# Linear attention and a gated convolution FFN on one core: one batch's q transposed on TensorE, one convolution moved to VectorE, a new order

## The chip, the cores and the metric

The kernel runs on 1 core of a Trainium2 chip. The metric is the device time of one execution in microseconds. Runs are compared by their median; the profile is of one further execution, and its span runs from the first to the last instruction.

## The reference

For each of 8 batches and 8 heads (576 tokens, 64 dims) linear attention without a softmax is computed, normed over the head dim, and all heads of a batch become one 576 x 512 matrix that goes through a gated FFN with a convolution over the tokens:

```python
kv  = einsum('bhsd,bhse->bhde', k, v)
out = einsum('bhsd,bhde->bhse', q, kv)
x   = out / sqrt(mean(out*out, -1) + 1e-6) * g_norm      # -> x[b, s, h*64+d], 512 wide
h   = maximum(x @ w_in, 0)                               # 512 -> 1024
c   = w0*h[s-1] + w1*h[s] + w2*h[s+1]                    # per feature, zero at the ends
y   = (h * sigmoid(c)) @ w_out                           # 1024 -> 512
```

Inputs and outputs are fp32 in HBM; the matmuls take bf16.

## The kernel before

All work is written as small steps, and one long text, `ORDER` (L67), lists the 690 of them. A loop (L797) calls each step in that order, and a chain of dependencies at the end (L807) keeps the instructions of each engine in it. So `ORDER` is the queue of every engine at once: a step that stands ahead of another is ahead of it on the engine that they share. What follows `@` are the buffer slots that the step takes (for PSUM, the first of the eight banks), and a `:1` moves a copy to the other of ScalarE and VectorE: for most steps no mark means ScalarE and `:1` VectorE, for `qc` and `qc0` it is the other way round.

The steps that matter here, with batch b first and token, head pair t, half u, feature block f or row block m behind it:

- `Lq`, `Lk`, `Lv` (L301) load and cast one batch on GpSimd's queue, two slots for each of q, k and v, so a load waits until the batch before last has been read. `Li` and `Lo` load quarters of w_in and halves of w_out. `pl` (L273) sets a selection matrix on GpSimd.
- `kv` (L349) multiplies k by v on TensorE; `kvc`, `kvn`, `ky` copy the result out of PSUM, `kx` by a transfer.
- q has to lie with the head dim on the partitions. Batches 0 to 3 transpose it on TensorE (`qt0`, `qt`; L380 in the rows); batch 4, the only one in `QP`, does so two tokens at a time (`qtp`, 12 products by the identity for each half, L388), and `qc` copies the result from PSUM. Batches in `QD` (5, 6, 7) use a transposing transfer instead, `dq` (L436), issued by SyncE: two for each batch.
- `ot` and `oq` multiply q by kv; `sq` squares on ScalarE, `oc` copies to fp32. Norms: batches 0 and 1 by `on`, `nl`, `mu0` (L562); the others by `ss` (L575), `ln`, `sl` on VectorE, `sp` (L603) and `mu` (L629), whose result is x. `fw` and `fr` bring batch 7's factors through HBM.
- `hm` (L640) is x @ w_in for one batch and 128 features, eight products of 288 columns; `ha` and `hb` are its two halves for features 2 and 3 of batch 1. `re` is the relu, on ScalarE (L646) or VectorE (L648).
- The convolution works in groups `CONV` (L64): 0 and 1 are batches 0 and 1 alone, 2, 3 and 4 two batches each. On VectorE it is `ta` (two scaled copies of h, L699 and L700), `aa` (their shifted sum, L706) and `ab` (plus h, L712), for two features at a time, in one of two `taps` buffers of two batches' size; a one-batch group leaves half of its buffer empty. On TensorE it is `cm` (L731): six products with diagonal matrices `dgw` that `dg` made. `sg` (L745 after `ab`, L742 after `cm`) is the sigmoid on ScalarE, `mg` (L751) multiplies h by it on VectorE.
- `om` (L761) is the product with w_out for 128 rows, in two halves for the pairs of batches in `SPLIT`; `ea` copies the row out, `st` stores it from SyncE's queue.
- `unread.n` and fill counts (L427) multiply a constant tile n times into a bank that nobody reads.

ScalarE loads an activation table ten times, wherever `ORDER` changes between norm steps and sigmoids.

In the order before, group 0 and group 1 do features 6 and 7 with `cm` and the other six on VectorE.

Of the kernel before, what the change touches and what calls it, by code (L numbers as in the profile page):

```python
# [67 lines left out]
pre@0,0,0 unread.10@0 qt0.0.0@0 ps pn pi ca.k.0 ca.v.0 kv.0.0.1@1 kvc.0.0.1.0:1@0 ct@2 qt0.0.1@3 qc0.0.0:1@0  # L68
kvc.0.0.1.1 ot.0.0@0 qc0.0.1:1 unread.3@4 kv.0.1.1@3 Lq.1.0@1 pg sq.0.0@0 on.0.0@4 al.x0@0 al.h1@0 nl.0.0@0 pc
dg.7:1 kvc.0.1.1.0:1 dg.6:1 unread.1@6 qt0.0.2@2 kvc.0.1.1.1:1 ot.0.1@6 unread.3@3 kv.0.2.1@3 sq.0.1@1 mu0.0.0  # L70
al.x1@1 Li.1 al.h0@1 kvc.0.2.1.0:1 Li.3 qc0.0.2:1@1 kvc.0.2.1.1:1 on.0.1@4 nl.0.1@1 qt0.0.3@2 Lv.1.0@1 ot.0.2@0
mu0.0.1 sq.0.2@2 qc0.0.3:1 unread.3@3 kv.0.3.1@4,5 kvc.0.3.1.0 on.0.2@6 kvc.0.3.1.1:1 nl.0.2@2 ot.0.3@4 mu0.0.2
sqh.0.3.0@3 unread.3@3 onh.0.3.0@6 sqh.0.3.1 onh.0.3.1 nlh.0.3.0@3 muh.0.3.0 Lk.1.0@1 qt.1.0@0 nlh.0.3.1 qc.1.0:1@2
muh.0.3.1 Li.0 hm.0.2@6 re.0.2 ta.0.2@0 hm.0.3@4 re.0.3 hm.0.6@6 Lq.1.2 ta.0.3 Lv.1.2 re.0.6 aa.0.1 hm.0.7@4 Lk.1.2
Lq.2.0@0 cm.0.6@6 re.0.7:1 sg.0.6@1 kv.1.0.2@0 cm.0.7@4 kvc.1.0.2.0:1@1 kvc.1.0.2.1 sg.0.7 ot.1.0@0 hm.0.1@6 ab.0.1
sq.1.0@4 re.0.1 qt.1.1@4 hm.0.0@2 on.1.0@6 mg.0.3 qc.1.1@3 ot.1.1@4 nl.1.0@4 re.0.0:1 sq.1.1@5 kv.1.2.2@2
kvc.1.2.2.0 ta.0.0@1 mu0.1.0 kvc.1.2.2.1 on.1.1@6 Li.2 ot.1.2@2 nl.1.1@5 ot.1.3@0 ta.0.1 sq.1.2@6 mu0.1.1 aa.0.0
# [5 lines left out]
sq.2.2@1 sg.0.4 oc.2.2@1 sg.0.5 sq.2.1@2 Lo.1 Lq.4.0@0 Lq.5.0@1 qc.3.0@2 ta.1.5 ot.2.3@4 re.1.1:1 sq.2.3@3 hm.1.0@6
oc.2.1 Lk.4.0@0 Lv.4.0@0 kv.3.0.4@2 re.1.0 ss.2@3 oc.2.3 mg.0.2 ln.8@0 aa.1.2 kvc.3.0.4.0:1@1 kvc.3.0.4.1:1 ab.1.2
unread.3@0 ot.3.0@4 ta.1.0@1 ot.3.1@6 sq.3.0@4 ot.3.2@0 ta.1.1 al.x2@0 oc.3.0@2 aa.1.0 sq.3.2@5 oc.3.2@3 sq.3.1@6
om.0.3.0@2 om.0.0.0@3 oc.3.1 sl.8@0 om.0.1.0@4 ot.3.3@0 om.0.1.4 ab.1.0 om.0.3.4 sq.3.3@7 oc.3.3 sp.2.1@6,0 ss.3@5
dq.5.0@3 ea.0.1@0 mu.2.1.0 Lk.5.0@1 mu.2.1.1 om.0.0.4 ea.0.3@1 ln.1@0 sp.2.0@4,6 mu.2.0.1 mu.2.0.0 dq.5.1@0
# [5 lines left out]
st.0.0 ab.2.2 ta.2.6@0 sg.2.5 re.3.1 re.3.2 ta.2.7 oq.4.3@6 oq.4.2@0 sg.2.4 re.2.3 kv.5.0.4@5 sq.4.2@2 Lv.7.0@0
Lk.7.0@0 om.0.6.4 om.0.5.0@2 aa.2.3 ab.2.3 Lk.6.0@1 Lv.6.0@1 kvn.5.0.4 sq.4.3@3 oc.4.2@0 mg.2.2 ky.5.0.4.0:1
ea.0.6@4 ss.4@3 dq.7.0@1 oc.4.3 ky.5.0.4.1:1 oq.5.0@0 oq.5.1@4 sq.5.0@4 ta.2.2@1 om.0.5.4 sq.5.1@5 oc.5.0:1@2
om.0.4.0@6 oc.5.1 ta.2.3 oq.5.3@0 oq.5.2@4 aa.2.1 om.0.8.0@7 ea.0.5@5 ab.2.1 sq.5.3@6 om.0.4.4 sq.5.2@7 ss.5 ln.2@0
om.0.8.4 hm.2.1@2 oc.5.2@3 ea.0.8@6 oc.5.3 re.2.1 sl.2@0 hm.2.0@4 sp.4.1@0,2 ea.0.4@7 om.0.7.0@7 re.2.0 mu.4.1.0
mu.4.1.1 sp.4.0@4,0 kv.7.0.4@6 mu.4.0.0 sg.2.2 mu.4.0.1 om.0.7.4 kvn.7.0.4:1 sg.2.3 ea.0.7@2 sp.5.0@4,2 hm.3.0@0
al.h2@1 re.3.0 kx.7.0.4.0 dq.7.1@4 mu.5.0.1 mu.5.0.0 hm.4.5@2 re.4.5 sp.5.1@6,4 hm.4.1@0 mg.2.1 mu.5.1.0 hm.4.2@2
mu.5.1.1 ta.2.0@1 sg.2.7 hm.4.0@6 hm.5.3@4 ta.2.1 re.4.1 sg.2.6 mg.2.3 kx.7.0.4.1 re.4.0 re.4.2 oq.7.0@0 re.5.3  # L100
kv.6.0.4@6 oq.7.1@4 sq.7.0@0 hm.5.2@2 oc.7.0@1 aa.2.0 Lq.6.0@1 hm.4.3@0 st.0.4 dq.6.0@2 sq.7.1@1 oc.7.1 re.5.2
hm.4.4@4 st.0.5 kvn.6.0.4:1 ab.2.0 ta.3.2@0 re.4.3 hm.5.6@0 st.0.1 ta.3.3 hm.5.4@2 hm.5.1@6 sg.2.1 sg.2.0 re.4.4
# [22 lines left out]
def kernel(  # L125
# [567 lines left out]
    @op  # L693
    def ta(c, f):
        h, n = span(c)
        if f % 2 == 0:
# [2 lines left out]
        nc.vector.tensor_scalar_mul(tap[:, 0, f % 2, :n, 8:8 + S], h[:, f], cwn[:, 0, f:f + 1])  # L699
        nc.vector.tensor_scalar_mul(tap[:, 1, f % 2, :n, :S], h[:, f], cwn[:, 2, f:f + 1])  # L700
# [145 lines left out]
```

## Time and profile before

| | us |
|---|---|
| median of 3 runs | 179.97 (179.6 to 180.15) |
| profiled execution, first to last instruction | 177.6 |
| the median over that span | 2.4 |
| last matmul ends, from the span's start | 174.3 |
| TensorE busy | 168.4 |
| ScalarE busy | 149.7 |
| VectorE busy | 139.5 |
| GpSimd busy | 30.8 |

No time of its own is listed for the profiled execution beside its span; the 2.4 us are what the timed runs have around it. In the rows PE is TensorE's matmul, PEld its weight load, DVE VectorE, ACT ScalarE, POOL GpSimd, SP SyncE. An engine's instructions overlap at their ends, so busy times are less than sums of durations. The granted TensorE clock is 1.000 in the mean. The loads keep the transfer engines busy until about 100 us.

### The profile page before, as it was taken

To read this page: it belongs to the slowest core of one execution; us is meant where nothing else is said; L and a number is where in the kernel's file an instruction comes from. 1 tells how busy PE (TensorE), PEld (TensorE's weight loads), DVE (VectorE), ACT (ScalarE), POOL (GpSimd) and SP (SyncE) were. 2 spreads that over 40 slices of the span, in tenths; PEclk is the share of its full clock that TensorE was granted. 3 is DMA by queue.
4 is the path that set the end of the run, shared out by engine and by line. 5 is a ranking of instruction groups with operands and counts; after the bars stand their busy time and mean duration, and the time that the engine had idled before them with its cause. 6 is when DMAs were issued, how large, how long until landed. Compare 5 with 4: busy or idle time off the path is not lost.

```text
span 177.6 us, 4060 instructions
## 1 busy us (share of the span) xinstructions
PE 168.4 (95%) x1641; PEld 101.3 (57%) x1660; DVE 139.5 (79%) x235; ACT 149.7 (84%) x233; POOL 30.8 (17%) x54
## 2 busy tenths in 40 slices
...
GB/s 155 188 183 197 200 204 201 205 203 206 205 204 203 198 192 139 174 203 198 160 201 179 293 128 0 53 219 263 21 160 0 4 0 143 152 82 99 258 352 219
DMA packets 36219, 29.49 MB, mean 166 GB/s; under 512 B 8528, under 2 KB 31720, under 8 KB 36200
## 3 DMA queue, kind: packets, MB, share of 16 engines
...
## 4 chain that ended last, share of the span: by engine, by line
PE 70%; DMA 20%; POOL 4%; ACT 2%; issue 2%; POOLq 0%; ACTq 0%
PE bank L761 33%; PE bank L640 27%; DMA v_sb<-in_v_dram 10%; DMA k_sb<-in_k_dram 7%; DMA q_sb<-in_q_dram 4%; PE bank L358 3%; PE bank L464 2%; POOL q_sb L241 1%; PE bank L603 1%; PE bank L575 1%; POOL v_sb L241 1%; POOL k_sb L241 1%; PE bank L776 1%; PE bank L731 1%; PE bank L388 1%
## 5 line engine op out<-in xcount | busy, mean ns | idle before, releaser
L640 PE MATMUL bank<-xT,w_in_sb 128*128 128x288 bf16 x496 | 64.5, 286 | 0.1
L761 PE MATMUL bank<-w_out_sb,h 128*128 128x512 bf16 x268 | 63.0, 379 | 1.1 <-issue 0.6
L640 PEld LDWEIGHTS <-w_in_sb 128*128 128x128 bf16 x496 | 47.6, 98 | 14.1 <-issue 0.5
L761 PEld LDWEIGHTS <-h 128*128 128x128 bf16 x280 | 26.3, 98 | 30.6 <-issue 1.9
L646 ACT ACTIVATE h<-bank 128x576 bf16<-128x576 f32 x61 | 37.9, 657 | 4.2 <-PE bank L640 3.9
L745 ACT ACTIVATE taps<-taps,cwn 128x1152 bf16<-128x1152 bf16 (+1 forms) x36 | 38.2, 1094 | 0.1
L341 ACT ACTIVATE row<-bank 128x512 f32<-128x512 f32 (+1 forms) x37 | 21.3, 598 | 12.3 <-PE bank L761 9.3
L751 DVE TENSOR_TENSOR h<-h,taps 128x2304 bf16<-128x2304 bf16 (+1 forms) x20 | 22.2, 1113 | 2.0 <-ACT taps L745 1.2
L706 DVE TENSOR_TENSOR taps<-taps 128x2304 bf16<-128x2304 bf16 (+1 forms) x18 | 20.9, 1160 | 0.4
L712 DVE TENSOR_TENSOR taps<-taps,h 128x2304 bf16<-128x2304 bf16 (+1 forms) x18 | 20.8, 1153 | 0.3
L699 DVE TENSOR_SCALAR taps<-h,cwn 128x1152 bf16<-128x1152 bf16 (+1 forms) x36 | 16.7, 463 | 2.5 <-ACT h L646 2.4
L493 ACT ACTIVATE sq<-bank 128x576 bf16<-128x576 f32 x28 | 17.9, 676 | 0.0
L700 DVE TENSOR_SCALAR taps<-h,cwn 128x1152 bf16<-128x1152 bf16 (+1 forms) x36 | 17.5, 487 | 0.0
L629 DVE SCALAR_TENSOR_TENSOR xT<-o,cw,bank 128x576 bf16<-128x576 f32 x20 | 15.3, 809 | 2.7 <-PE bank L603 2.5
L341 ACT ACTIVATE o<-bank 128x576 f32<-128x576 f32 x22 | 15.0, 694 | 0.0
L213 ACT ACT_TABLE_LOAD x10 | 12.8, 1283 | 2.5 <-issue 2.4
L301 POOL DMA_DIRECT2D q_sb<-in_q_dram x8 | 6.2, 772 | 31.4 <-PE bank L388 16.6
L427 PE MATMUL bank<-fill 128*128 128x512 bf16 x25 | 9.0, 480 | 1.7 <-DVE fill L228 1.5
L358 PEld LDWEIGHTS <-k_sb 96*64 96x64 bf16 x384 | 7.3, 114 | 4.0 <-issue 2.6
L358 PE MATMUL bank<-v_sb,k_sb 96*64 96x64 bf16 x384 | 8.5, 199 | 1.0 <-DMA k_sb<-in_k_dram 0.7
L301 POOL DMA_DIRECT2D k_sb<-in_k_dram x8 | 6.1, 758 | 14.4 <-PE bank L358 12.5
L562 DVE SCALAR_TENSOR_TENSOR xT<-bank,cw,root 128x576 bf16<-128x576 f32 x7 | 5.6, 815 | 1.8 <-ACT root L542 1.7
...
## 6 DMA issues: line engine op xcount, KB each, us to landing
...
```

The costliest lines, as they stand in the source:

```text
L341: nc.scalar.activation(to, fr, AX.Copy)
L358: nc.tensor.matmul(ps[i][i * D:(i + 1) * D, t - t0, :], k_sb[:, 2 * t + i, r * D:(r + 1) * D], v_sb[:, 2 * t + i, r * D:(r + 1) * D], star ...
L493: nc.scalar.activation(in_order(b, s), product(b, t), AX.Square)
L640: nc.tensor.matmul(ps[:, e, :HS], w_in_sb[:, t, f * P:(f + 1) * P], x[:, t, e * HS:(e + 1) * HS], start=(t == 0), stop=(t == NT - 1))
L646: nc.scalar.activation(to, fr, AX.Relu)
L699: nc.vector.tensor_scalar_mul(tap[:, 0, f % 2, :n, 8:8 + S], h[:, f], cwn[:, 0, f:f + 1])
L700: nc.vector.tensor_scalar_mul(tap[:, 1, f % 2, :n, :S], h[:, f], cwn[:, 2, f:f + 1])
L706: nc.vector.tensor_add(tap[:, 1, :, :n, :S], tap[:, 0, :, :n, 7:7 + S], tap[:, 1, :, :n, 1:1 + S])
L712: nc.vector.tensor_add(y, y, h[:, 2 * j:2 * j + 2])
L745: nc.scalar.activation(y, y, AX.Sigmoid, scale=cwn[:, 1, f:f + 1])
L751: nc.vector.tensor_mul(h, h, T["tap", c, j][:, 1, :, :n, :S])
L761: nc.tensor.matmul(T["om", p, m], h[:, f, m * P:(m + 1) * P], w_out_sb[:, f, :], start=(f == 0), stop=(f == NF - 1))
```

## The change

Batch 5 moves from `QD` to `QP`: `dq.5.0` and `dq.5.1` go, `qtp.5.0`, `qtp.5.1`, `qc.5.0` and `qc.5.1` come. `cm.1.6` and `cm.1.7` go; `ta.1.6`, `ta.1.7`, `aa.1.3` and `ab.1.3` come, and `sg.1.6` and `sg.1.7` now read what VectorE made. The two `taps` buffers of two batches become one tile of four units of one batch each; a one-batch group takes one unit, a two-batch group two neighbours. The rest is `ORDER`: all steps are listed anew, with new slots, and 44 evictions (copies and relus) change between ScalarE and VectorE. Of the 27 fill products that `unread` issues, 17 are left.

```diff
-QD = (5, 6, 7)
-QP = (4,)
+QD = (6, 7)
+QP = (4, 5)
...
+    def units(n):
+        s = slots.pop(0)
+        return taps[:, s:s + n].rearrange("p b k f w -> p k f b w")
...
-    taps = [consts.tile([P, 2, 2, 2, TW], BF16, name=f"taps{i}") for i in range(2)]
+    taps = consts.tile([P, 4, 2, 2, TW], BF16, name="taps")
...
-        for t in taps:
-            nc.vector.memset(t[:, 0, :, :, 7:8], 0.0)
-            nc.vector.memset(t[:, 1, :, :, S:S + 1], 0.0)
+        nc.vector.memset(taps[:, :, 0, :, 7:8], 0.0)
+        nc.vector.memset(taps[:, :, 1, :, S:S + 1], 0.0)
...
     def ta(c, f):
         h, n = span(c)
         if f % 2 == 0:
-            T["tap", c, f // 2] = taps[slots.pop(0)]
+            T["tap", c, f // 2] = units(CONV[c][1])
...
             if f % 2 == 0:
-                T["tap", c, f // 2] = taps[slots.pop(0)]
+                T["tap", c, f // 2] = units(CONV[c][1])
```

The stretch of `ORDER` from `kv.1.2.2` on, before and after, where the prediction follows it step by step (left out steps are marked):

```diff
-kv.1.2.2@2 kvc.1.2.2.0 ta.0.0@1 mu0.1.0 kvc.1.2.2.1 on.1.1@6 Li.2 ot.1.2@2 nl.1.1@5 ot.1.3@0 ta.0.1 sq.1.2@6 mu0.1.1 aa.0.0
-unread.1@6 on.1.2@6 sq.1.3@7 ab.0.0 nl.1.2@6 mu0.1.2 on.1.3@4 nl.1.3@7 Lk.2.0@0 qt.2.0@6 sg.0.3 qt.2.1@4 mu0.1.3
-ha.1.2@2 hb.1.2 ...
+kv.1.2.2@0 ta.0.0@2 kvc.1.2.2.0 mu0.1.0 kvc.1.2.2.1 Lq.2.0@0 on.1.1@6 nl.1.1@1 ot.1.2@2 sq.1.2@0 ta.0.1 mg.0.3 hm.0.5@0 mu0.1.1
+on.1.2@6 re.0.5 ot.1.3@4 hm.0.4@0 aa.0.0 nl.1.2@0 sq.1.3@0 on.1.3@6 re.0.4 nl.1.3@1 mu0.1.2 sg.0.2 ha.1.3@2 ab.0.0
+ta.0.4@1 ha.1.2@0 ta.0.5 sg.0.1 mu0.1.3 hb.1.3 hb.1.2 ...
...
-kv.3.0.4@2 re.1.0 ss.2@3 oc.2.3 mg.0.2 ln.8@0 aa.1.2 kvc.3.0.4.0:1@1 kvc.3.0.4.1:1 ab.1.2 unread.3@0 ot.3.0@4 ...
-om.0.2.0@2 Lv.5.0@1 sg.1.5 sg.1.4 qtp.4.0@0 cm.1.6@6 qc.4.0@4 mg.1.2 ea.0.0@2 hm.2.5@4 sl.1@0 hm.2.2@0 sg.1.1
-om.0.2.4 re.2.5 sg.1.6@0 re.2.2 ea.0.2@3 sg.1.0 sp.3.0@6,4 cm.1.7@0 mu.3.0.1 mu.3.0.0 hm.2.4@2 hm.2.7@6 sg.1.7
-sp.3.1@0,4 mg.1.0 re.2.4 mg.1.3 kv.4.0.4@2 mu.3.1.0 mu.3.1.1 ... hm.3.4@0 hm.3.5@4 ...
+kv.3.0.4@6 ta.1.6@0 ta.1.7 ss.2@7 kvc.3.0.4.0@0 kvc.3.0.4.1 aa.1.2 re.1.1:1 Lo.1 ta.1.0@3 ln.8@0 qt.3.1@0 ot.3.1@2 ...
+ab.1.2 qc.3.1@0 oc.3.0@2 ot.3.2@0 ta.1.1 Lq.4.0@0 om.0.1.0@7 ... aa.1.0 sl.8@0 sq.3.3@3 ab.1.1 ... aa.1.3 ss.3@3 sp.2.1@0,4
+Lv.4.0@0 ab.1.0 ea.0.1@0 ab.1.3 om.0.2.4 mu.2.1.0 ln.1@0 mu.2.1.1 ... sp.2.0@6,0 om.0.0.4 sg.1.4 ea.0.2@2 mu.2.0.0
+ea.0.0@3 mu.2.0.1 qtp.4.0@4 qc.4.0:1@0 hm.2.5@6 re.2.5 qtp.5.1@0 sg.1.0 sg.1.7 sl.1@0 sg.1.3 qtp.5.0@2 qc.5.1@1
+Lk.4.0@0 hm.2.2@4 sp.3.0@0,6 qc.5.0@2 re.2.2 sg.1.6 mu.3.0.0 hm.2.4@2 hm.2.7@0 sg.1.2 mu.3.0.1 re.2.4:1 sp.3.1@4,6
+mu.3.1.0 Lk.5.0@1 mu.3.1.1 kv.4.0.4@2 re.2.7 sg.1.5 kvn.4.0.4 sg.1.1 qtp.4.1@0 hm.3.5@4 ...
```

More of the change, by code (lines that the diff above doesn't have):

```diff
@@ L67 @@
 ORDER = """
[L68 to L77, printed above, removed]
@@ L83 @@
[L83 to L87, printed above, removed]
@@ L93 @@
[L93 to L102, printed above, removed]
@@ L118 @@
-om.3.0.0@4 st.2.3 ea.3.6@6 ea.3.1@0 st.3.6 st.3.3 st.3.1 st.2.4 st.2.5 om.3.5.4 om.3.2.4 om.3.7.0@2 st.2.6 ea.3.4@6
-st.2.0 eh.3.8.0@7 st.3.4 om.3.0.4 ea.3.5@0 om.3.7.4 oh.3.8.1 ea.3.2@3 ea.3.0@4 ea.3.7@1 st.3.5 st.1.4 sh.3.8.0
-st.3.2 st.3.0 st.3.7 eh.3.8.1 sh.3.8.1
+pre@0,0,0 ca.k.0 pi ca.v.0 unread.10@6 qt0.0.0@0 al.h1@0 kv.0.0.1@1 kvc.0.0.1.0@0 ct@2 kvc.0.0.1.1 al.x0@0 qt0.0.1@3
+pg unread.3@6 kv.0.1.1@2 qc0.0.0:1@0 dg.7:1 kvc.0.1.1.1 Lq.1.0@1 Li.1 ot.0.0@0 pc sq.0.0@0 al.x1@1 kvc.0.1.1.0:1
@@ new lines @@
+unread.3@6 on.0.0@4 qc0.0.1:1 qt0.0.2@2 nl.0.0@0 qc0.0.2@1 ot.0.1@6 unread.1@3 kv.0.2.1@3 sq.0.1@0 mu0.0.0 on.0.1@4
+kvc.0.2.1.0 al.h0@1 Li.3 kvc.0.2.1.1:1 ot.0.2@0 nl.0.1@1 sq.0.2@0 qt0.0.3@2 ps qc0.0.3 mu0.0.1 on.0.2@4 kv.0.3.1@3,2
+Lv.1.0@1 Lk.1.0@1 kvc.0.3.1.0:1 kvc.0.3.1.1 dg.6:1 ot.0.3@6 nl.0.2@0 pn mu0.0.2 sqh.0.3.0@0 sqh.0.3.1 onh.0.3.0@2 Li.0
+nlh.0.3.0@1 onh.0.3.1 muh.0.3.0 nlh.0.3.1 qt.1.0@4 muh.0.3.1 Lq.1.2 hm.0.2@0 re.0.2 hm.0.3@2 qc.1.0@0 ta.0.2@0
+hm.0.6@4 re.0.3 re.0.6:1 hm.0.7@0 re.0.7 kv.1.0.2@2 cm.0.6@4 sg.0.6@1 Lv.1.2 cm.0.7@0 Lk.1.2 kvc.1.0.2.0:1@0
@@ new lines @@
+kvc.1.0.2.1:1 sg.0.7 ot.1.0@2 hm.0.0@6 hm.0.1@4 Li.2 ta.0.3 aa.0.1 ab.0.1 re.0.0:1 qt.1.1@0 re.0.1:1 Lk.2.0@0 sq.1.0@0
+on.1.0@6 qc.1.1@1 ot.1.1@4 nl.1.0@0 sq.1.1@0 kv.1.2.2@0 ta.0.0@2 kvc.1.2.2.0 mu0.1.0 kvc.1.2.2.1 Lq.2.0@0 on.1.1@6
+nl.1.1@1 ot.1.2@2 sq.1.2@0 ta.0.1 mg.0.3 hm.0.5@0 mu0.1.1 on.1.2@6 re.0.5 ot.1.3@4 hm.0.4@0 aa.0.0 nl.1.2@0 sq.1.3@0
+on.1.3@6 re.0.4 nl.1.3@1 mu0.1.2 sg.0.2 ha.1.3@2 ab.0.0 ta.0.4@1 ha.1.2@0 ta.0.5 sg.0.1 mu0.1.3 hb.1.3 hb.1.2 Lv.2.0@0
+aa.0.2 sg.0.0 ab.0.2 re.1.2 re.1.3:1 qt.2.0@4 sg.0.3 qt.2.1@6 kv.2.0.4@2 sg.0.5 hm.1.4@0 mg.0.0 qc.2.0@0 ta.1.2@2
@@ new lines @@
+kvc.2.0.4.0@0 Lq.3.0@1 sg.0.4 kvc.2.0.4.1 hm.1.7@4 pl qc.2.1@1 ot.2.0@6 ta.1.3 re.1.4 re.1.7 sq.2.0@0 mg.0.2 Lk.3.0@1
+hm.1.5@2 ot.2.2@0 oc.2.0@0 aa.1.1 hm.1.6@4 sq.2.2@1 oc.2.2@1 Lv.3.0@1 ta.1.4@1 re.1.5:1 mg.0.1 ot.2.3@6 sq.2.3@2
+qt.3.0@2 Lo.0 ta.1.5 re.1.6 hm.1.0@0 ot.2.1@4 oc.2.3 qc.3.0@1 sq.2.1@3 hm.1.1@2 oc.2.1 re.1.0 kv.3.0.4@6 ta.1.6@0
+ta.1.7 ss.2@7 kvc.3.0.4.0@0 kvc.3.0.4.1 aa.1.2 re.1.1:1 Lo.1 ta.1.0@3 ln.8@0 qt.3.1@0 ot.3.1@2 ot.3.0@4 om.0.3.0@6
+sq.3.0@0 ab.1.2 qc.3.1@0 oc.3.0@2 ot.3.2@0 ta.1.1 Lq.4.0@0 om.0.1.0@7 sq.3.1@1 sq.3.2@2 oc.3.1 Lq.5.0@1 ot.3.3@4
```

55 lines of the change are left out of this document (33 added, 22 removed).

## The prediction

> **What bounds the kernel now.** I read the page first (busy shares), then the chain of waits in order of time, then busy time by stage, then the groups by shape and the timelines of single engines.
>
> ```profile
> PE 168.4 (95%) x1641; PEld 101.3 (57%) x1660; DVE 139.5 (79%) x235; ACT 149.7 (84%) x233; POOL 30.8 (17%) x54
> ```
>
> TensorE is the fullest, and the stages say where it is not full. Columns: window, its length, busy time of PE, PEld, DVE, ACT, POOL, clock, DMA share, GB/s. I cut at the starts of kv.1.2, kv.3, kv.4 and kv.6.
>
> ```profile
> 16.60:27.00 10.40, 9.66 (x116) 7.00 (x114) 6.90 (x15) 9.28 (x14) 3.86 (x5) 1.00 1.33 202
> 27.00:30.80 3.80, 2.56 (x36) 1.34 (x38) 3.57 (x8) 3.50 (x8) 2.52 (x12) 1.00 1.36 200
> 30.80:45.90 15.10, 14.70 (x230) 11.23 (x232) 14.85 (x29) 15.03 (x26) 4.66 (x7) 1.00 1.31 205
> 45.90:63.90 18.00, 17.71 (x179) 9.92 (x183) 15.65 (x29) 17.19 (x29) 1.64 (x2) 1.00 1.29 201
> 63.90:97.00 33.10, 32.57 (x412) 20.98 (x414) 30.74 (x44) 31.79 (x51) 4.74 (x6) 1.00 1.32 183
> 97.00:141.00 44.00, 43.84 (x369) 27.76 (x367) 40.76 (x56) 42.64 (x65) 0.00 (x0) 1.00 0.41 116
> ```
>
> From 30.8 on TensorE has hardly a hole, and ScalarE is as full beside it; VectorE has some slack from 45.9 on. So a microsecond of TensorE work taken out there is a microsecond won, if no other engine or load is late. Up to 46 us loads set the dates, as the chain shows (start, length, what):
>
> ```profile
> 28.67 17.11 DMA v_sb<-in_v_dram
> 45.78 0.14 issue
> 45.91 0.95 PE bank L358 x48
> ...
> 56.54 0.51 PE bank L388 x12
> 57.05 0.74 PE bank L731 x6
> ...
> 60.85 0.85 PE bank L731 x6
> ...
> 64.82 0.62 PE bank L388 x12
> ```
>
> The v of batch 3 lands at 45.78 and kv.3 starts at once. The last four lines price the exchange: a dgw convolution (L731) took 0.74 and 0.85 us of TensorE, a two-token transpose step (L388) 0.51 and 0.62.
>
> **The change, part by part.** VectorE and ScalarE overlap the end of an operation with the next one's start, so I add from start to start, not by mean durations:
>
> ```profile
> 36.07 0.76 DVE L706 TENSOR_TENSOR taps<-taps 128x1152 bf16<-128x1152 bf16 x1
> 36.87 0.76 DVE L712 TENSOR_TENSOR taps<-taps,h 128x1152 bf16<-128x1152 bf16 x1
> 37.54 0.75 DVE L751 TENSOR_TENSOR h<-h,taps 128x1152 bf16<-128x1152 bf16 x1
> 38.21 0.36 DVE L699 TENSOR_SCALAR taps<-h,cwn 128x576 bf16<-128x576 bf16 x1
> 38.49 0.36 DVE L700 TENSOR_SCALAR taps<-h,cwn 128x576 bf16<-128x576 bf16 x1
> 38.77 0.36 DVE L699 TENSOR_SCALAR taps<-h,cwn 128x576 bf16<-128x576 bf16 x1
> ```
>
> A one-batch sum or product thus costs 0.67 in a row, a tap 0.28. In the same way: relu, copy and square on ScalarE 0.53, output row 0.48; relu, copy and qT copy on VectorE 0.67.
>
> *Exchange on TensorE.* cm.1.6 and cm.1.7 go: 0.74 + 0.85 = 1.59 off. qtp.5.0 and qtp.5.1 come: 0.51 + 0.62 = 1.13 on. Both lie between kv.3 and kv.4, where TensorE sets the pace. Sum: -0.46.
>
> *Filler products.* Ten of 27 go. Those ahead of 30 us stand in waits, so 0. The last three (46.8 to 47.8) cover the eviction of kv.3; qt.3.1 (0.65), moved behind kv.3, covers it now. 0.
>
> *VectorE.* Batch 1's features 6 and 7: four taps and two sums, 4 x 0.28 + 2 x 0.67 = 2.5. Two qT copies of batch 5: 1.3. Counting the choices in the order, 30 evictions go from ScalarE to VectorE (+17.7 there, -15.3 here) and 14 the other way (-6.1, +6.0). VectorE +15.5, from 133.8 to 149.3 added up; ScalarE -9.0, from 143.1 to 134.1. No output row was copied by VectorE before: ten are now, priced between ScalarE's 0.48 and the 0.67 of a 576-wide copy; I take 512/576 x 0.67 = 0.60, so 4.8 to 6.7 for all; six of them fall into the last 30 us, where VectorE had nothing to do. The two-batch taps now lie in two units with a gap; the one-batch forms already read h with gaps at the same rate (1152 in 0.67, 2304 in 1.27), so I price this at 0. That all four units are one buffer orders nothing more: the PSUM `bank` is one tile too, and its parts are written and read side by side now.
>
> *Transfers.* qtp.5.1 puts a new wait on TensorE, for q of batch 5, with hm.2.2 and all behind it; it comes near 58.5, and that q lands at 56.3: 0. The two dq.5 transposes go:
>
> ```profile
> 56.40 7.41 SPq L436 DMA_TRANSPOSE qT<-q_sb  x2
> ```
>
> Beside them k and v of batch 5 landed at 66.78 and 71.85, 9.2 us for two loads, where k and v of batch 4 took 2.9 and 3.5. That frees about 3 us of transfers, but kv.5 started at 75.96, 4 us after its data: worth 0. Loads moved past each other: Li.2 goes ahead of Lq.2.0, and pl (1.4 us of POOL memsets) ahead of Lk.3.0 and Lv.3.0. Those waited 14.5 and 17.1 us from issue to landing, so the queue hides it and Lv.3.0 still lands at 45.8. Lq.5.0 is released by qt.3.1 and goes out near 48 instead of 43.5, with q of batch 4 still on its way until 53.4: 0. Batch 6's q now comes ahead of its k and v, and three dq steps fall among Lv.7, Lv.6 and Lk.6. Six loads of 3 us from 68 and 1.6 us for each dq put Lk.6 at 88 to 91; kv.6 comes at about 91.7. Cover of 1 us; gone, it costs up to 1.
>
> *From kv.1.2 (27.04, on its k load) to kv.3.* hm.0.5 and hm.0.4 (0.98 each) now fill waits. But mu0.1.3, for which hb.1.3 and hb.1.2 wait, queues behind more. ScalarE ends kvc.1.2 at 28.2, then has nl, sq, re, nl, sq, re, nl (3 x 0.64 + 4 x 0.53 = 4.0) and some 0.4 of waits: nl.1.3 ends at 32.6. VectorE gets nl.1.2 at 30.9 and does mu0.1.2, ab.0.0, ta.0.4, ta.0.5, mu0.1.3: 0.73 + 0.67 + 2 x 0.56 + 0.73 = 3.25, so 34.2. The two hb end at 35.3, against 34.05 now, with 0.63 more work done (1.96 more hm, 1.33 of qt.2 not yet): 0.6 behind. Ahead of kv.3 then stand 10.0 to 10.4 us of TensorE work: 45.3 to 45.7. The load's 45.8 hides it by 0.1 to 0.5; if not, each tenth late is a tenth lost.
>
> *From kv.3 to kv.4.* Two terms. ScalarE holds TensorE up now: sp.2.1 starts at 53.60 when oc.3.3 ends (53.66), and cm.1.7 waits likewise for re.2.2. Against back-to-back starts of its matmuls I count 0.8 us of such holes between 47 and 61; with ScalarE lighter they go: -0.8 (0 to -1.2). VectorE becomes tight: 19.4 us of its work stand between the two marks (15.8 before) against 17.4 of TensorE's. It enters ahead by 1.2 (its mu0.1.3 by the sums above, carried on). The ends that matter: hm.2.5 needs mu.2.0.1, after 12.8 us of VectorE work from kv.3 against 11.2 of TensorE's, and hm.3.5 needs mu.3.1.1, 19.4 against 18.1. With the 1.2 ahead and 0.1 per hand-over, each waits about 0.3: +0.6 (0 to 2.0).
>
> *After kv.4.* By the same sums VectorE is behind TensorE nowhere by more than it has in hand: thinnest at sp.4.1 and hm.4.5 (0.7 left), hm.7.2 and om.2.2.0 (0 to 0.4 left). 0, upper bound +1. The tail (last matmul to end, 3.3) stays.
>
> Sum: -0.46 - 0.8 + 0.6 = -0.66 on the profiled span of 177.6, so 176.9. The median 179.97 lies 2.4 above the span; with that kept, 179.3. A run set of this kernel can tell about 0.3%, 0.54 us, from no change; the forecast is just past it.
>
> **Rivals.**
> *Everything is paid back (no change).* TensorE reaches kv.3 after 45.8, or kv.6 waits for its k. For: margins of 0.1 to 0.5 and 1. Against: both come from rounded sums with no lost cover found. Half a microsecond back: 179.5 to 180.5. Chance 0.20.
>
> *VectorE becomes the bound (slower).* Place: hm.2.5 and hm.3.5. If VectorE comes to kv.3 with nothing in hand instead of 1.2, both waits together are the full 19.4 - 17.4 = 2.0; with 0.5 more at om.2.2.0: -0.46 - 0.8 + 2.5 = +1.2, 181.2. It decides when mu.2.0.1 ends after about 58.4 us. For: VectorE is already 14.85 of 15.10 busy from 30.8 on, and gains 15.5. Against: ten of the copies fall where it idled. Chance 0.28.
>
> *ScalarE was the real pace (much faster).* ScalarE is 42.64 of 44.00 busy from 97 on. If TensorE's small gaps there (1 to 2 us from 64 to 130) were its doing, 1 us more goes: 178.2. Against: those gaps stand at changes between kinds of matmul, whoever waits. Chance 0.13.
>
> *The clock falls (slower).* Granted clock is 1.00 in every window; the first ten fillers, from 1.47 on, took 4.45, later ones 0.22 each. With seven fewer between 6 and 30 us TensorE idles more. If it fell back once, the first 2.2 us of hm.0 would take twice that; kv.1.2's wait (0.72) and 0.2 of margin at kv.3 leave 1.3: 180.6. Chance 0.06, as no gap that I foresee there is above 1.5 us. [...]
>
> **Numbers.** Forecast itself (178.8 to 179.4): 0.33. With the much faster case, faster is 0.46; same 0.20; slower 0.34. Most likely 179.3. Range 177.8 to 181.6: from the fast rival with the full -1.2 to VectorE's case with 0.4 on it.
>
> **What would show it.** Right: L731 x12 instead of x24, L388 x48, DMA_TRANSPOSE x4; kv.3 at 45.8; hm.2.5 near 57.5; PE's last matmul at 173.6; VectorE busy near 155 (139.5 + 15.5), ScalarE near 141. Wrong: kv.3 after 46.2; waits of PE L640 or L603 on DVE xT above 0.6 us in sum; kv.6 on a load; a clock below 1 after 10 us; or ScalarE's rows with idle and PE still as late.

## The result and the profile after

The changed kernel is slower: median 180.91 us (13 runs) against 179.54 us for the kernel before (13 runs beside it), a ratio of 1.0076 with a 95% interval of 1.0048 to 1.0104. Executions more than 1.5% above the fastest of their kernel count in the medians, but neither in the ratios nor in the ranges of times and clocks given below. The profiled execution took 180.17 us with a span of 178.4; it is one of the quickest of its set, so the traces show only 0.8 us of the loss of 1.37 (178.4 against 177.6), and the mean clocks in the table below bear on the rest.

Every timed execution on record is 1.7 to 1.9 us longer than its own span. The 2.4 us that stand between the old median and the old span are therefore not all around the span: about 0.6 of them are there because the profiled execution of the kernel before was quicker than the median.

The page of the changed kernel: busy times, the row of TensorE's granted clock in 40 slices, and the shares of the chain of waits.

```profile
PE 166.1 (93%) x1645; PEld 101.3 (57%) x1662; DVE 154.4 (87%) x257; ACT 140.3 (79%) x217; POOL 30.6 (17%) x54
...
PEclk9997899999999999999999999999999999999999
...
PE 67%; DVE 19%; ACT 5%; DMA 3%; issue 3%; POOL 1%; POOLq 0%; DVEq 0%; ACTq 0%
```

The shares of the chain before:

```profile
PE 70%; DMA 20%; POOL 4%; ACT 2%; issue 2%; POOLq 0%; ACTq 0%
```

The work moved as summed: VectorE 154.4 (155 forecast), ScalarE 140.3 (141). (The forecast's -9.0 for ScalarE is -9.3 by its own two terms, and 9.4 went.) Two things are new. The clock dips in the fourth and fifth slice, and the chain runs through loads (DMA) for 3% of the span instead of 20%, and through VectorE for 19%, with hardly a break from 33.4 to 59.3 us.

The same windows as before, in which the changed kernel's steps lie about 1 us later (window, its length, busy time of PE, PEld, DVE, ACT, POOL, clock, DMA share, GB/s):

```profile
16.60:27.00 10.40, 10.35 (x113) 7.66 (x114) 6.81 (x14) 6.40 (x10) 3.09 (x4) 0.87 1.35 201
27.00:30.80 3.80, 2.99 (x62) 2.24 (x63) 3.69 (x8) 3.47 (x7) 2.50 (x11) 1.00 1.32 202
30.80:45.90 15.10, 13.44 (x200) 9.70 (x201) 14.88 (x30) 14.65 (x25) 3.26 (x5) 1.00 1.30 204
45.90:63.90 18.00, 17.64 (x213) 10.56 (x215) 17.64 (x34) 17.73 (x30) 4.74 (x6) 1.00 1.28 204
63.90:97.00 33.10, 32.62 (x442) 21.31 (x443) 31.55 (x47) 32.62 (x53) 3.83 (x5) 1.00 1.15 185
97.00:141.00 44.00, 43.84 (x333) 27.79 (x334) 43.09 (x60) 37.33 (x55) 0.00 (x0) 1.00 0.33 99
```

The first row has a clock of 0.87, the third a TensorE that is 1.26 us less busy than before. From 45.9 on TensorE is as full as it was, with VectorE nearly full beside it.

TensorE's timeline, first of the changed kernel, then of the kernel before (start, length, instructions, and in brackets what an idle time ahead of them waited for):

```profile
16.82 1.17 PE L382 MATMUL bank<-ident,q_sb 96*64 96x96 bf16 x24
17.92 4.80 PE L642 MATMUL bank<-xT,w_in_sb 128*128 128x288 bf16 x32
...
28.59 0.57 PE L360 MATMUL bank<-v_sb,k_sb 96*64 96x64 bf16 x24 [0.26 <-DVE qT L345]
...
36.01 0.90 PE L665 MATMUL bank<-xT,w_in_sb 128*128 128x288 bf16 x6 [1.13 <-DVE xT L564]
...
47.02 0.95 PE L360 MATMUL bank<-v_sb,k_sb 96*64 96x64 bf16 x48
```

```profile
15.96 0.70 PE L380 MATMUL bank<-ident,q_sb 96*64 96x96 bf16 x24
16.59 4.09 PE L640 MATMUL bank<-xT,w_in_sb 128*128 128x288 bf16 x32
...
27.04 0.57 PE L358 MATMUL bank<-v_sb,k_sb 96*64 96x64 bf16 x24 [0.72 <-DMA k_sb<-in_k_dram]
```

The first four hm of batch 0 start 1.33 us later, and the same 32 products take 4.80 us instead of 4.09. kv.1.2 then starts at 28.59 instead of 27.04 and waits no more for its load, and kv.3 at 47.02 instead of 45.91, with no wait for its load either. The loss is there, ahead of kv.3; behind it the changed kernel is the faster one.

All kernels that were run, by the same marks. Starts of three steps are from the span's start; "rest" is from the start of kv.3 to the end of the last matmul; the clock is the mean of the timed executions, lowest to highest; the ratio is to the kernel before.

| kernel | hm.0.2 | kv.1.2 | kv.3 | rest | clock | median us | ratio (95%) |
|---|---|---|---|---|---|---|---|
| before | 16.59 | 27.04 | 45.91 | 128.35 | 0.990 to 1.000 | 179.5 to 179.8 | 1 |
| changed | 17.92 | 28.59 | 47.02 | 127.55 | 0.978 to 0.990 | 180.91 | 1.0076 (1.0048 to 1.0104) |
| e1 | 18.09 | 28.06 | 46.48 | 127.51 | 0.996 to 1.000 | 179.37 | 0.9968 (0.9944 to 0.9992) |
| e2 | 17.58 | 27.66 | 46.83 | 128.09 | 0.978 to 1.000 | 180.38 | 1.0032 (0.9995 to 1.0068) |
| e3 | 17.91 | 27.87 | 46.29 | 127.51 | 0.990 to 1.000 | 179.42 | 0.9991 (0.9962 to 1.0020) |
| e4 | 17.39 | 27.47 | 47.78 | 127.82 | 0.986 to 1.000 | 181.94 | 1.0105 (1.0065 to 1.0145) |
| e5 | 16.64 | 26.60 | 45.57 | 127.56 | 0.990 to 1.000 | 178.97 | 0.9953 (0.9922 to 0.9984) |
| e6 | 17.85 | 27.82 | 46.24 | 134.71 | 0.981 to 0.990 | 184.86 | 1.0287 (1.0237 to 1.0337) |
| e7 | 17.31 | 27.28 | 45.71 | 129.10 | 0.996 to 1.000 | 182.44 | 1.0135 (1.0087 to 1.0183) |
| e8 | 17.85 | 29.05 | 47.48 | 127.50 | 0.995 to 1.000 | 180.39 | 1.0031 (1.0004 to 1.0058) |
| e9 | 17.05 | 27.80 | 46.23 | 127.50 | 0.969 to 1.000 | 179.75 | 1.0017 (0.9986 to 1.0048) |
| e10 | 16.47 | 26.55 | 45.60 | 130.19 | 0.997 to 1.000 | 182.19 | 1.0151 (1.0128 to 1.0174) |
| e11 | | | | | 0.990 to 1.000 | 178.99 | 0.9963 (0.9940 to 0.9985) |
| e12 | 16.90 | 26.98 | 45.79 | 129.53 | 0.999 to 1.000 | 180.40 | 1.0070 (1.0046 to 1.0093) |

(The marks of e11 are left out: in its profiled execution hm.0.2 waited 1.41 us for its load of w_in, and the clock fell once, to 0.989 in the mean.)

### The profile page after: what moved, and what is told of

Read it like the earlier page. It is cut to its first block, busy times and chain, and to the rows that moved or that the text cites. A ratio compares the mean times of both kernels' runs of the same rounds, so it can differ in the third digit from the quotient of the medians.

```text
span 178.4 us, 4089 instructions
## 1 busy us (share of the span) xinstructions
PE 166.1 (93%) x1645; PEld 101.3 (57%) x1662; DVE 154.4 (87%) x257; ACT 140.3 (79%) x217; POOL 30.6 (17%) x54
## 4 chain that ended last, share of the span: by engine, by line
PE 67%; DVE 19%; ACT 5%; DMA 3%; issue 3%; POOL 1%; POOLq 0%; DVEq 0%; ACTq 0%
PE bank L763 30%; PE bank L642 27%; DVE qT L345 3%; DMA v_sb<-in_v_dram 3%; DVE xT L564 2%; ACT taps L747 2%; DVE taps L702 2%; PE bank L360 2%; DVE taps L714 2%; DVE taps L708 2%; DVE taps L701 2%; DVE xT L631 2%; DVE h L753 1%; DVE h L650 1%; PE bank L466 1%
## 5 line engine op out<-in xcount | busy, mean ns | idle before, releaser
L642 PE MATMUL bank<-xT,w_in_sb 128*128 128x288 bf16 x496 | 65.8, 288 | 0.2
L747 ACT ACTIVATE taps<-taps,cwn 128x1152 bf16<-128x1152 bf16 (+1 forms) x38 | 39.8, 1083 | 5.1 <-DVE taps L714 4.9
L648 ACT ACTIVATE h<-bank 128x576 bf16<-128x576 f32 x51 | 32.0, 660 | 7.5 <-PE bank L642 7.2
L343 ACT ACTIVATE row<-bank 128x512 f32<-128x512 f32 (+1 forms) x27 | 15.4, 588 | 12.2 <-PE bank L763 9.8
L708 DVE TENSOR_TENSOR taps<-taps 128x2304 bf16<-128x2304 bf16 (+1 forms) x19 | 21.6, 1136 | 0.3
L701 DVE TENSOR_SCALAR taps<-h,cwn 128x1152 bf16<-128x1152 bf16 (+1 forms) x38 | 17.4, 458 | 1.8 <-ACT h L648 1.7
L702 DVE TENSOR_SCALAR taps<-h,cwn 128x1152 bf16<-128x1152 bf16 (+1 forms) x38 | 17.7, 465 | 0.0
L343 ACT ACTIVATE o<-bank 128x576 f32<-128x576 f32 x21 | 14.2, 683 | 0.0
L650 DVE TENSOR_SCALAR h<-bank 128x576 bf16<-128x576 f32 x13 | 9.6, 753 | 1.1 <-PE bank L642 0.9
L345 DVE COPY row<-bank 128x512 f32<-128x512 f32 x10 | 6.7, 686 | 4.3 <-PE bank L763 4.3
L345 DVE COPY qT<-bank 128x1152 bf16<-128x1152 bf16 (+1 forms) x11 | 8.2, 752 | 1.5 <-PE bank L382 1.3
```

What stands on the lines that cost most here:

```text
L343: nc.scalar.activation(to, fr, AX.Copy)
L345: nc.vector.tensor_copy(to, fr)
L642: nc.tensor.matmul(ps[:, e, :HS], w_in_sb[:, t, f * P:(f + 1) * P], x[:, t, e * HS:(e + 1) * HS], start=(t == 0), stop=(t == NT - 1))
L648: nc.scalar.activation(to, fr, AX.Relu)
L708: nc.vector.tensor_add(tap[:, 1, :, :n, :S], tap[:, 0, :, :n, 7:7 + S], tap[:, 1, :, :n, 1:1 + S])
L747: nc.scalar.activation(y, y, AX.Sigmoid, scale=cwn[:, 1, f:f + 1])
```

## The experiments

### The clock: fill products put in and taken out

**e1**, on the changed kernel:

```diff
-on.0.1@4 ... ot.0.2@0 ... on.0.2@4 ... ot.0.3@6 ... onh.0.3.0@2
+on.0.1+1@4 ... ot.0.2+1@0 ... on.0.2+2@4 ... ot.0.3+3@6 ... unread.2@2 onh.0.3.0@2
```

> The changed kernel with nine fill products put back into waits between 12 and 16.5 us (1 in on.0.1, 1 in ot.0.2, 2 in on.0.2, 3 in ot.0.3, 2 ahead of onh.0.3.0). Theory (the clock falls to half for 3.41 us because TensorE is thin there, and that is most of the loss): mean clock 1.000, hm.0.2 near 17.6, kv.3 near 45.9 instead of 47.0, time 178.9 to 179.5, that is 1.3 to 2 us under the changed kernel. Rival A (the new work itself, VectorE's above all, is the loss): clock 1.000, but kv.3 still near 47 and the time 180.3 to 181. Rival B (it is the start-up order on VectorE and ScalarE): a gain of at most 0.5 us, 180.2 to 180.6.

Measured: 179.37, and a clock of 0.996 to 1.000 in all twelve executions. Nine products that compute nothing take 1.5 us off the changed kernel (1.9 by the ratios to the kernel before, which stood at other medians beside other sets) and put it below the kernel before (0.9968, 0.9944 to 0.9992). hm.0.2 came no earlier (18.09, where 17.6 was expected), the four hm at full clock made up 0.5 us. All executions of the changed kernel have a clock of 0.990 or less: those at 0.986 to 0.990 took 180.14 to 181.02, those at 0.978 to 0.980 took 181.23 to 182.48. So the fill products, and with them the clock, are the larger part of the loss, and the late start of hm.0 is something else.

**e2**, on the kernel before:

```diff
-unread.1@6 qt0.0.2@2 ... unread.3@3 kv.0.2.1@3 ... unread.3@3 kv.0.3.1@4,5 ... unread.3@3 onh.0.3.0@6 ... unread.1@6 on.1.2@6
+unread.1@6 qt0.0.2@2 ... unread.1@3 kv.0.2.1@3 ... kv.0.3.1@4,5 ... onh.0.3.0@6 ... on.1.2@6
```

> The kernel before with only those fill products left that the changed kernel has ahead of 30 us (17 instead of 27 less the last three, which stay: 18 in all). Theory: the clock falls once, to a mean of about 0.99, and the time goes up by 0.7 to 1.7 us on the kernel before, to 180.2 to 181.2, with nothing else changed. Rival A and B (clock not decisive): within 0.3 us of the kernel before, 179.3 to 179.8, whether the clock falls or not.

Measured: 180.38 against 179.62, ratio 1.0032 (0.9995 to 1.0068), an interval that just takes in no difference. Nine products are out, and 15 are left ahead of 30 us, two fewer than in the changed kernel. Ten executions sort themselves by their clock: 179.10 to 179.95 in the four at 0.998 or 1.000, 179.90 to 180.63 in the four at 0.990, 181.62 and 181.78 in the two at 0.98. One period of 3.41 us at half clock, as the changed kernel's trace has it from 15.97 to 19.39, takes 0.0096 off the mean, so by their means these are none, one and two of them, and one costs about 1 us. No instruction differs between these executions, so the step is not one of the program; but the kernel before spreads from 179.0 to 180.8 at a clock of 0.997 and more, so that "about 1 us" is rough. Six of these ten have a clock of 0.990 or less, against none of 28 of the kernel before beside them.

**e9** takes the fill products out of e5 (below) in the same way; 15 are left ahead of 20 us, not 17.

> The run with the first 17 us of the kernel before and hm.0.2 in bank 6, less eight of its fill products between 9 and 16 us (17 left ahead of 20 us instead of 23... that is 10, 3, 1 and 1). Theory (the fill products hold the clock, whatever the order): the clock falls again in most executions, mean 0.98 to 0.99, and 1.2 to 2 us are lost on that run's 178.97: 180.2 to 181.0. Rival (the start-up order itself makes TensorE full enough): clock 1.000, 178.8 to 179.2.

Measured: 179.75, 0.8 over e5 (1.1 by the ratios), below the range expected; the clock is below 0.991 in all executions but one. The direction is the theory's, the size smaller.

The stretches around the falls of the clock. In the changed kernel's trace the record of the granted clock is at full from 5.73 us, at half from 15.97 to 19.39, 3.41 us long, and at full from there to the end. Here and in e9 the half clock came 10.24 us (three times 3.41) after the record's full clock began, in e2 3.41 us after; it lasted 3.41 us in each, and 6.83 in e6. I cut the windows at multiples of 3.41 us from the start of full clock in each execution. The changed kernel:

```profile
9.15:12.56 3.41, 2.84 (x35) 1.27 (x33) 2.00 (x6) 2.84 (x7) 3.31 (x6) 1.00 1.30 197
12.56:15.97 3.41, 1.85 (x29) 1.12 (x31) 3.20 (x12) 2.44 (x5) 1.88 (x3) 1.00 1.41 198
15.97:19.39 3.42, 3.21 (x33) 2.03 (x33) 2.52 (x5) 1.36 (x4) 1.90 (x3) 0.50 1.34 201
19.39:22.80 3.41, 3.41 (x37) 2.58 (x37) 1.41 (x3) 1.35 (x3) 1.20 (x2) 1.00 1.35 201
```

The second of these windows in e1, whose own multiples of 3.41 us lie 0.16 us later:

```profile
12.56:15.97 3.41, 3.01 (x35) 1.46 (x34) 3.28 (x11) 2.30 (x4) 2.31 (x4) 1.00 1.41 200
```

The same for e2 and for e9:

```profile
4.60:8.02 3.42, 2.09 (x43) 1.21 (x41) 1.82 (x8) 1.08 (x3) 3.42 (x6) 1.00 1.23 182
8.02:11.43 3.41, 3.41 (x30) 1.26 (x29) 2.23 (x12) 1.73 (x3) 3.41 (x6) 0.50 1.27 186
```

```profile
8.43:11.84 3.41, 2.20 (x34) 0.96 (x31) 2.03 (x8) 1.93 (x3) 3.17 (x5) 1.00 1.28 183
11.84:15.26 3.42, 1.70 (x30) 0.97 (x31) 1.46 (x4) 3.18 (x7) 2.35 (x5) 1.00 1.32 189
15.26:18.67 3.41, 3.35 (x33) 2.12 (x33) 1.50 (x3) 2.33 (x5) 1.57 (x3) 0.50 1.35 198
```

A stretch with 1.85, 2.09 or 1.70 us of TensorE work (the number behind the comma) is followed by one at 0.50; after the one with 2.20, in e9, the clock is still 1.00. In e1 the window that was thin holds 3.01. In the changed kernel and in e9 the thin stretch is one that lacks fill products. In e2's trace it is not: the products taken out stood behind 10 us, and from 4.60 to 8.02 TensorE waited 1.07 us for the load of q. So that trace shows a thin stretch with half clock behind it, and for e2 only the count of executions above shows what the products do. No border can be read from these: two stretches of e4, with 2.10 and 2.02 us, were followed by full clock, and so was one with 2.06 us each in e5 (32.88 to 36.29) and in e12 (4.21 to 7.63). The two of e4 and the one behind them:

```profile
26.40:29.81 3.41, 2.10 (x34) 1.12 (x32) 3.09 (x7) 3.28 (x7) 2.99 (x12) 1.00 1.36 198
29.81:33.23 3.42, 2.02 (x16) 1.34 (x17) 1.19 (x2) 1.29 (x3) 1.55 (x3) 1.00 1.32 204
33.23:36.64 3.41, 2.46 (x19) 1.58 (x17) 3.17 (x7) 3.32 (x6) 0.00 (x0) 1.00 1.32 204
```

### The start: the order of the first 17 us

**e3** is the changed kernel with everything up to muh.0.3.1 in the order before, fill products too; the rest follows in the changed order:

```diff
-pre@0,0,0 ca.k.0 pi ca.v.0 unread.10@6 qt0.0.0@0 al.h1@0 kv.0.0.1@1 ... nlh.0.3.1 qt.1.0@4 muh.0.3.1
+pre@0,0,0 unread.10@0 qt0.0.0@0 ps pn pi ca.k.0 ca.v.0 kv.0.0.1@1 ... nlh.0.3.1 qc.1.0:1@2 muh.0.3.1 Li.0
 Lq.1.2 hm.0.2@0 ...
```

> The changed kernel with the order and the fill products of the kernel before up to muh.0.3.1 (17.2 us there), all the rest as changed. Theory (clock and late start together are the loss): clock 1.000, hm.0.2 at 16.6, kv.3 at 45.8 to 46.1, time 178.5 to 179.0, below the kernel before by 0.5 to 1.0 and a little below the run with fill products alone. Rival A (VectorE's new work between 25 and 36 us is the loss): hm.0.2 at 16.6, yet kv.3 at 46.6 or later, 179.8 to 180.6. Rival B (start-up order): as the theory, but then the run with fill products alone gains little.

Measured: 179.42, no better than e1. hm.0.2 started at 17.91 and not at 16.6: its bank 0 holds qt.1.0 in the order before, and it waited for ScalarE to copy that out (1.14 us, to 17.87). The graft had made a wait of its own, so it told nothing of the start order.

**e5** is e3 with that taken away:

```diff
-hm.0.2@0
+hm.0.2@6
```

> As the run with the first 17 us of the kernel before, with hm.0.2 in bank 6 and not in bank 0, where it waited until 17.91 for ScalarE to copy qt.1.0 out. Theory (the rest of the loss is the late start of hm.0): hm.0.2 at 16.6 to 16.9, kv.1.2.2 near 27, kv.3 at 45.7 to 46.0, 178.4 to 178.9. Rival A (VectorE between 25 and 36 us, or the loads, hold TensorE up whatever the start): hm.0.2 earlier by 1 us, but kv.3 still at 46.2 or later and the time within 0.2 of 179.4.

Measured: 178.97 (0.9953, 0.9922 to 0.9984), the fastest kernel here. Its TensorE timeline:

```profile
16.64 4.09 PE L642 MATMUL bank<-xT,w_in_sb 128*128 128x288 bf16 x32
...
26.60 0.57 PE L360 MATMUL bank<-v_sb,k_sb 96*64 96x64 bf16 x24 [0.26 <-DVE qT L345]
...
45.57 0.95 PE L360 MATMUL bank<-v_sb,k_sb 96*64 96x64 bf16 x48 [0.47 <-DMA v_sb<-in_v_dram]
```

With hm.0.2 on time kv.3 waits for its load again, and everything behind it comes 1.45 us earlier than in the changed kernel. e9 against the changed kernel (179.75 and 180.91) gives the worth of the old start without its fill products, 1.1 us by the ratios, whose intervals just touch; e5 against e1 gives 0.3 with them, which the intervals don't tell from nothing, although in the two traces kv.3 comes 0.91 us earlier. The two causes overlap: either cure shortens the same late chain.

**e4** takes the order before up to kv.1.2.2 (27.0 us) into the changed kernel.

> The changed kernel with the order and fill products of the kernel before up to kv.1.2.2 (27.0 us there), the rest as changed. Theory: kv.1.2 at 27.0, clock 1.000, 178.5 to 179.0, no better than with the first 17 us alone, as the order between 17 and 27 us costs nothing. Rival A, in the form that the changed order from 17 to 27 us holds TensorE up (kv.1.2 waits for VectorE's qc.1.1): 0.4 to 1 us faster than the run with the first 17 us alone.

Neither came: 181.94, with kv.3 at 47.78 in the profiled execution. Two of the six executions, the profiled one among them, were at full clock (180.83 and 181.19); the other four, at 0.986 to 0.991, took 181.87 to 182.12, again about 1 us more. The chain of waits shows another wait of the graft:

```profile
18.71 12.21 DMA w_in_sb<-in_moe_w_in_dram
30.92 0.04 issue
30.96 1.17 PE bank L642 x8
```

`Li.2` went out at 18.7 and landed at 30.92, when hm.0.5 was waiting for it: the changed order has hm.0.5 ahead of kv.2 and `Li.2` ahead of `Lq.2.0`, the old start has `Lq.2.0` first.

**e8** moves three VectorE steps of e1 out of the start-up chain:

```diff
-ps ... dg.6:1 ... pn ... muh.0.3.1
+... muh.0.3.1 dg.6:1 ps pn
```

> The changed kernel with the nine fill products, and three VectorE steps that stand in its busy chain of 12 to 16.5 us (dg.6, ps, pn, together some 1.8 us) moved behind muh.0.3.1. Theory (the late start is VectorE's chain up to sqh and muh): hm.0.2 at 16.9 to 17.3 instead of 18.09, kv.3 at 45.8 to 46.2, 178.5 to 179.1. Rival (another engine or the load of v ends the start as late): hm.0.2 no more than 0.3 earlier, time within 0.2 of 179.4.

Measured: 180.39, a microsecond slower than e1; hm.0.2 moved by 0.24 only. In the chain of waits the three steps stand in front of batch 1's qT copy instead:

```profile
17.56 0.94 DVE xT L537 x2
18.50 0.81 DVE dgw L723 x3
19.35 0.43 DVE spread L288
...
20.34 0.67 DVE qT L345
21.05 2.12 PE bank L642 x16
```

hm.0.6 takes the bank that this copy frees. Where I put them they only moved the wait. Whether they would help behind the copy was not run, so which step of the new order makes hm.0.2 late stays open.

### The exchange: one part undone, one part done alone

**e6**, on e1: batch 5's q by transfer again.

```diff
-QD = (6, 7)
-QP = (4, 5)
+QD = (5, 6, 7)
+QP = (4,)
...
-qtp.5.1@0 ... qtp.5.0@2 qc.5.1@1 ... qc.5.0@2
+dq.5.1@1 dq.5.0@2
```

> The changed kernel with the nine fill products, and batch 5's q transposed by the two transfers again (dq.5.1 and dq.5.0 in the place of qtp.5.1), the VectorE convolution kept. Theory (TensorE is the pace from kv.3 to kv.4, the transfers delay only loads that have cover): 1.1 us of TensorE and 1.3 of VectorE less, kv.4 at 62.8 to 63.3 instead of 63.9; but the two loads of batch 5 land near 67 and 72 and those of batches 7 and 6 some 3 us later, so kv.7 or kv.6 waits: 178.6 to 179.6. Rival (the transfers cost nothing): 178.0 to 178.4. Rival (the transfer was the dear part and its removal the gain): 180 or more, with kv.5 on its load.

Measured: 184.86, 5.5 us over e1, beyond every theory. TensorE's waits and the chain:

```profile
PE bank L360 <- DMA k_sb<-in_k_dram: 3.9, 1, 3.9
```

```profile
58.72 13.99 DMA qT<-q_sb
...
77.10 19.23 DMA k_sb<-in_k_dram
96.33 0.04 issue
96.38 1.49 PE bank L360 x24
```

The transfers end at 72.7; only then do the loads of batches 7 and 6 go out on GpSimd's queue, because the first of them takes the slot of batch 5's q, and the k of batch 6 lands at 96.33, where it landed at 89.48 in the changed kernel. kv.6, at 92.4 in e1, waits 3.9 us, and the clock is at half from 95.2 to 102.1 (a mean of 0.981 over this execution's span of 184.2). In the changed order, which puts batch 7's q ahead of the other loads, the transfers cost over 5 us; an order made for them was not run.

**e7**, on e1: features 6 and 7 of batch 1 by TensorE again.

```diff
-ta.1.6@0 ta.1.7 ... aa.1.3 ... ab.1.3 ... hm.2.5@6 re.2.5 ... sg.1.7 ... sg.1.6
+cm.1.6@2 cm.1.7@0 sg.1.6@0 hm.2.5@6 sg.1.7 re.2.5
```

> The changed kernel with the nine fill products, and batch 1's features 6 and 7 convolved by TensorE again (cm.1.6 and cm.1.7 ahead of hm.2.5), batch 5's q kept on TensorE. Theory (TensorE is the pace and VectorE holds it up a little at hm.2.5 and hm.3.5): 1.59 us of TensorE more, 0.3 to 0.6 of waits less: 180.3 to 181.0. Rival (VectorE is the bound from kv.3 to kv.4): 178.9 to 179.5, no slower than with fill products alone.

Measured: the rest behind kv.3 is 129.10 against 127.51, 1.59 more, the price of the products put back. The profiled execution took 180.40, as expected; the median of all is 182.44, beyond both ranges, and what the other executions lose at a clock of 0.996 to 1.000 no profile here shows.

**e10**, on the kernel before: only q of batch 5 on TensorE.

```diff
-dq.5.0@3 ... dq.5.1@0 ... ta.2.4@1
+qtp.5.1@6 qc.5.1@0 qtp.5.0@4 qc.5.0@3 ta.2.4@1
```

> The kernel before with batch 5's q transposed on TensorE (qtp.5.1, qtp.5.0 ahead of ta.2.4, near 67 us) in place of the two transfers, and nothing else. Theory (in the old order no load is late, so the transfers cost nothing and the transposes 1.13 us of TensorE and 1.3 of VectorE): 0.6 to 1.3 us slower than the kernel before, 180.2 to 181.0. Rival (the transfers were on the path of the loads in the old order too): 0.3 us faster or more, 179.4 or less.

Measured: 182.19, 1.5% or 2.7 us slower, twice the theory's price. In the trace, which is of the quickest execution, the rest is 1.84 longer; 1.13 are the transposes, by the prediction's price. For the other 0.7 the chain of waits goes through VectorE from 67.85 to 80.45 without a stop, the two qT copies in front of it and batch 5's kvx copies, for which oq.5 waits, at its end:

```profile
67.85 0.57 DVE qT L342
68.42 0.10 issue
68.52 0.75 DVE qT L342
...
80.02 0.43 DVE kvx L342
80.45 0.04 issue
80.50 0.44 PE bank L463 x7
```

**e12**, on the kernel before: only the convolution on VectorE, in a tile of four units.

```diff
-cm.1.6@6 ... cm.1.7@0 ... sg.1.6@0
+ta.1.1 ta.1.6@3 ta.1.7 ... ab.1.0 aa.1.3 ab.1.3 ... sg.1.6
```

> The kernel before with batch 1's features 6 and 7 convolved on VectorE (ta.1.6 and ta.1.7 behind ta.1.1, aa.1.3 and ab.1.3 behind ab.1.0) in place of cm.1.6 and cm.1.7, the taps buffers in one tile of four units, and nothing else. Theory (TensorE is the pace from kv.3 to kv.4 and VectorE has 2.3 us of slack there): 0.8 to 1.6 us faster than the kernel before, 178.0 to 178.8. Rival (VectorE has no slack where it counts, or the tap units cost): 179.4 or more.

Measured: 180.40, slower by 0.7%, although TensorE has 1.59 us less to do. The rest is 1.18 longer, and TensorE's waits between 46 and 66 us name VectorE, at sp.2.0 and at hm.2.5 and hm.2.7, and ScalarE once, at hm.2.4:

```profile
PE bank L605 <- DVE xT L631: 0.7, 1, 0.7
PE bank L642 <- DVE xT L631: 0.6, 2, 0.4
PE bank L642 <- ACT row L343: 0.4, 1, 0.4
```

The gap in the taps cost nothing here: a shifted sum of two batches took 1362 ns in the mean in this run and in the kernel before.

**e11** adds four fill products to e5, in TensorE's wait near 33 us (`unread.4@6 hb.1.3`).

> The run with the first 17 us of the kernel before and hm.0.2 in bank 6, with four more fill products ahead of hb.1.3, in TensorE's wait of 1.29 us near 33 us, where a stretch of 3.41 us was 0.60 busy. Theory (that stretch lets the clock fall in some executions): mean clock 1.000 or 0.996 and up in all of them, 178.4 to 178.9, and a narrower spread. Rival (the clock is safe there): within 0.15 us of 178.97, spread as before.

Measured: 178.99 against 178.97, the same. So there is no sign that this wait costs the clock; 0.990 still occurs, as in e5.

## Why the prediction was wrong

**The step that failed is where the sum begins.** The working started "From kv.1.2 (27.04, on its k load)" and took the first 27 us as they were. kv.1.2 came at 28.59. From there the sum held: kv.1.2 to kv.3 took 18.43 us (18.3 to 18.7 by the prediction's figures), and the rest took 127.55 instead of 128.35, 0.80 off against 0.66 forecast. The 1.55 us ahead of it, less what the old load waits hid, put kv.3 1.11 later and turned the sign. e5 brings kv.1.2 back to 26.60 and kv.3 to its load; its span of 176.8 is the forecast's 176.9, and by the ratio it is 0.84 us faster than the kernel before (0.3 to 1.4).

**The tail and the 2.4 us** are two smaller terms. The tail was to stay at 3.3; it took 3.80, which is 0.50 of the 0.81 by which the spans differ. Over all traces here it takes 3.3 to 3.9, with the old end of the order and with the new one, so no run shows that the change made it longer. The forecast of 179.3 carries the 2.4 us; with 1.8, what the timed runs have around their own spans, the same sum gives 178.7.

**"Those ahead of 30 us stand in waits, so 0"** is the first half of that step. The fill products fill waits, and that was counted as if they also did nothing. e1 and e9 price them at 1.5 to 1.9 and 0.8 to 1.1 us.

**The start-up order** is the other half. It was never walked through. In the profile before, TensorE waited 0.72 us at kv.1.2 for a load, which is cover for that much lateness and no more. The batch 0 chain of copies, squares and norms is alternately on VectorE and ScalarE, and the changed order brought it to hm.0.2 1.33 us later, more than the cover. e5 shows that the old order up to there undoes this, but no run shows which step of the new order causes it.

**The clock rival** named what then showed, a fall of the clock with fewer fill products, and at a fair price (180.6; the executions at 0.986 to 0.990 took 180.1 to 181.0, and those at 0.978 to 0.980, two periods at half clock by the mean, 181.2 to 182.5), but it had only a chance of 0.06, "as no gap that I foresee there is above 1.5 us". The longest wait in the thin stretch was 0.59 us, so the gaps were even shorter than foreseen; they add up to 1.56 of its 3.41 us, and half clock came behind the 1.85 us of matmuls that were left. That the longest single gap is what to look at was the author's estimate, and no run shows it.

**VectorE as the bound** was priced at +0.6 at hm.2.5 and hm.3.5, and ScalarE's holes at -0.8, although the prediction's own row has TensorE busy for 17.71 of the 18.00 us from 45.90 to 63.90. kv.3 to kv.4 took 17.43 us instead of 17.96; of these 0.53 the exchange is 0.46 by its prices, so the two terms together came to -0.07, where -0.2 was forecast. TensorE's list of waits from 46 to 66 us names neither VectorE nor ScalarE, before and after. The other 0.27 came behind kv.4, where 0 was forecast. That the total comes so near the forecast is partly luck. Whether the two terms were near nothing or cancelled stays open, as the chain of waits runs through VectorE up to 59.1 us, and hm.2.5 started 11.75 us behind kv.3, as forecast (57.5 against 45.8). e12 shows that the rival was real for the convolution alone in the old order; which part of the new order keeps TensorE from waiting there no run separates.

**Transfers "worth 0"** held for the forecast but not as a price of the part: e6 shows that the new order's loads rely on the transfers being gone. "Lk.6 at 88 to 91" landed at 89.48, with kv.6 at 92.92.

Of the signs named: L733 x12, L390 x48 and DMA_TRANSPOSE x4 were right, and so were the busy times of VectorE and ScalarE; hm.2.5 at 58.77 and the last matmul at 174.6 came about 1 us later than named, as kv.3 did. "kv.3 after 46.2" and "a clock below 1 after 10 us" were the two that called it wrong, and both came true.
